# Deeper tile buffers and a new instruction order in a linear-attention and gated-MLP kernel on one core

## Chip, cores and metric

The kernel runs on one core of one Trainium2 chip. The metric is the device time of one execution in microseconds (us). Work on the core is spread over TensorE (PE), VectorE (DVE), ScalarE (ACT) and GpSimd (POOL); SyncE (SP) only issues transfers.

## What is computed

The input x has 2048 rows of 448 numbers in bfloat16. Two blocks follow each other, each with a layer norm in front and a residual addition behind:

```python
q, k, v = split(norm(x) @ wqkv)                 # 16 heads of 28
pq, pk = q @ w_phi, k @ w_phi                   # per head
phi_q = concat(softmax(pq), softmax(-pq))       # the same for phi_k
kv = phi_k^T v;  z = sum(phi_k over rows)       # per head
h = x + ((phi_q @ kv) / (phi_q @ z + 1e-6)) @ wo
h2 = h + (sigmoid(norm(h) @ w_gate) * (norm(h) @ w_up)) @ w_down   # 1792 hidden
```

## The kernel before, in words

The rows are cut into 16 tiles t of 128. Everything is one graph of tasks (class `_Graph`): a task has a name such as `("phi", 3)`, an engine or a choice of engines, one function that issues its instructions, and a list of tasks that it needs. `ORDER` (line 40) is a list of 902 numbers and fixes the order: number // 32 is the task by its place of creation, number % 4 says which of its allowed engines runs it, and number // 4 % 8 which PSUM banks it gets. `stored` (line 129) reads it, and `emit` (line 250) turns it into one in-order queue for each engine, with semaphore waits in front of an instruction where a task that it needs is on another engine or in a DMA. No engine skips a waiting instruction, SP's queue of transfers included. The bank gates are part of the waits: a product may write a bank pair only once the tasks that read its former content have ended (`until`).

The stages, with the names that the prediction uses:

- Opening. x, w_qkv's K, V and Q parts and w_phi are loaded (L461). PE runs `fill` products on zeros (L988, `NFILL` of them). `kT`/`WkT` (L540, L425) transpose the K weights, `Wp` on POOL or DVE (L524) spreads w_phi over the heads of a block, `wM`/`W2` (L555, L425) fold both into Wk and later Wq.
- Norm of x. Per tile `bst`, `agg` (bn_stats, bn_aggr, DVE, L583 and L585); per batch of tiles `ve` (L586), `rstd` (a power, POOL, L588), `mm`, `nm` (L591, L593); then `xn` (L602 or L603, ACT or DVE) writes the normalised tile into one of `NXP` slots of `xn_pad`. Tiles 0 to 3 are transposed by PE (`xP`, L613, with the copy `xT`, L425), the others two at a time by a DMA that SP issues (L621).
- K and V, and the key features. `pa`, `pb` (L637) are the first four and last three steps of a tile's K and V products, run as pairs on the two row halves of the array into a bank pair. `ekp`, `ekm` (ACT, L659 and L657) take exp of plus and minus K into one of `NEK` slots of `ek`; `v1` copies V into one of `NV` slots. `sa` (L667, POOL or DVE, written here as half_s) adds the two halves of each head, `ss` (L673) reduces, `rs` (L682) inverts, `phi` (L684) multiplies into one of `NPHI` slots, all but some `sa` on DVE. `kv` (PE, L696) accumulates phi and V over all tiles in bank 4, and `kvz` (L751) copies it out.
- Query features. `qa`, `q` (L736) for each of 4 chunks of 512 rows and 2 group pairs, `eqp`, `eqm` (ACT, L746).
- Read-out. `num` (PE, L772) per tile, `ocp` (L425, ACT or DVE, into opm), then on DVE per pair of tiles `rSm`, `rr`, `b`, `c`, `rd`, `o`, `od` (L788 to L819), a transpose `oT` (by PE for pair 0: `oP`, L808; by a DMA for the others, L821), `woa`, `wo_` (L833), and `h` (L863) or, for pair 0, `wr` and `hc` (L841, L856).
- Second norm. `bst2`, `agg2`, `ve2` (L871), `rstd2` (POOL, L873), `hn` (L877), `hT`.
- Gate/up and down. `ga`, `gu` (L934) into two banks, `sig` (ACT tanh, L943), `hh` (DVE, L951), `dn` (L968), `fin` (L975), store (L978). The gate and up weights (`wg`, `wu`, L461) come by eight SP loads, each behind a stage of the K products and behind the load two places before it in their list.

A slot of a buffer is written again only after its last reader: `xn` waits for the transpose `NXP` tiles back, `ekp` for the `phi` `NEK` back, `phi` for the `kv` `NPHI` back, `v1` for the `kv` `NV` back.

Of the kernel before, what the change touches and what calls it, by code (L numbers as in the profile page):

```python
# [5 lines left out]
dt = mybir.dt  # L6
ALU = mybir.AluOpType
# [3 lines left out]
P = 128  # L11
D = 448
H = 16
DH = 28
# [15 lines left out]
FIRST = [(0, 0), (0, 1), (0, 2), (0, 3), (1, 0), (1, 2), (1, 3)]  # L30
SECOND = [(1, 0), (1, 1), (1, 2), (1, 3), (0, 0), (0, 1), (0, 3)]
NWARM = 1
NFILL = 14

O_FIRST = [(0, 0), (0, 1), (0, 2), (0, 3), (1, 0), (1, 1), (1, 2)]
O_SECOND = [(1, 0), (1, 1), (1, 2), (1, 3), (0, 0), (0, 1), (0, 2)]
# [1 line left out]


ORDER = """  # L40
544 576 0 480 1152 609 224 737 128 28416 160 640 96 28448 352 801 192 28480 768 256 448 28512 384 896 28544
992 28576 1952 832 28608 28640 960 1984 2017 2112 28672 2048 673 28704 2144 705 2080 28736 2336 2176 928 28768
2208 2272 864 1184 1088 2368 2304 1316 2240 1216 2720 1120 1384 1344 1260 288 2656 1409 4144 2400 1588 512
1281 4160 2432 1440 1636 2592 1600 4072 9632 1472 2464 1520 28800 2496 1665 28832 4096 4204 1537 2528 4276
4225 1056 2624 4576 2688 2560 4289 2752 2785 3104 2848 2816 4608 3168 10272 3040 4516 5824 1024 2881 5536 2913
4712 2945 5568 3136 3200 3072 4320 2976 4544 3232 5632 4736 3264 5792 3008 5664 5888 4640 5696 6304 4352 5601
320 4672 6368 3297 5728 6336 5856 1760 5920 3328 1700 6080 1832 3616 5760 1793 3744 3360 4772 6048 3392 6112
3425 3680 6144 1888 3456 4800 5952 1856 3776 3648 4384 6400 3552 4832 1728 6176 6560 4904 5984 6592 10304 3488
4864 6208 6656 10176 6432 4928 6624 10208 3712 3584 6464 6848 4964 3809 6240 6816 6496 3520 6016 6272 3873
6881 6912 6528 7072 4416 4992 7136 6688 3840 7104 5024 6944 7392 10240 6720 5096 1921 6976 9664 3904 7360 6752  # L50
5056 9696 7328 7169 5120 3936 7008 10408 7616 3969 7584 7200 7424 4448 6784 7840 7040 7232 7648 10432 7680
7456 7904 5216 7488 7872 7264 10464 5160 7520 4032 7712 7936 5248 5184 7744 10496 9728 7776 7296 7552 4001
8096 7808 8161 4480 8128 5284 7968 8384 8352 5352 8193 10336 8416 8448 8224 5312 10144 8000 5376 8256 416 8608
8032 10532 8640 8672 8705 8864 8064 8480 10560 8896 8288 8928 5476 9792 10592 8736 8960 9760 5416 8512 8544
10624 5504 8768 5440 8992 9376 8800 10788 9408 9152 9024 9473 9120 8320 8576 9056 9184 8832 10816 9440 9504
9216 10656 9536 10848 9248 11048 9568 10880 9280 10688 9312 9088 10720 9344 9824 9600 9856 11072 11424 10752
10368 11524 12524 11104 11553 11456 11488 12545 12452 12480 13216 11584 13292 11616 11136 11648 10916 12576
13312 11680 11176 12608 12640 9888 13248 14060 10944 11712 12672 14080 11200 11744 10976 12704 11904 13344
11864 12736 11804 11232 13376 12768 11873 12800 11808 11008 13408 11936 13440 11264 13996 14756 13472 11968
13504 14016 11304 13536 12032 13568 12096 14112 14828 14784 12064 11328 12128 14144 12160 12000 14176 12836  # L60
12192 14848 12224 14208 15584 12864 12288 15616 12256 12408 12896 12348 13600 12353 14240 12416 12928 15524
13632 15552 14272 17836 13664 11360 17856 18084 14880 17888 17952 12992 11392 18112 17920 17984 13696 18476
9920 18144 18016 13024 18600 12960 14304 13728 13056 14336 18048 18496 13088 18176 18624 13760 18528 18208
18656 18560 18340 18688 18240 13792 13152 16364 9952 18272 18728 13825 13120 16384 18368 18304 13856 13184
18752 14912 18400 18976 13920 18784 16300 18432 19008 13888 14372 18816 19040 13952 14944 16320 17064 14400
19072 14976 9984 19232 14432 18860 17088 19264 18880 16416 19492 18912 19368 18944 19520 15008 16448 19392
19552 20076 19424 19584 15648 20196 15040 15072 19456 15104 20096 14464 19944 15680 20128 10016 19296 20224
19328 10048 20160 19968 20256 20448 20000 20032 20588 20288 15144 16480 17124 15712 15168 10080 17152 20608
15200 10112 20480 20640 20708 20672 20512 15744 19112 19820 15232 16512 20736 20544 19136 15776 20768 19840
16544 19168 21344 19200 15808 20328 19872 20800 19904 21220 14528 20352 15296 20844 15264 16576 20384 14496  # L70
15328 20416 21248 15360 15392 14560 20864 21280 15840 15456 21480 15872 20896 21312 20928 21376 14593 20964
14624 21408 21100 14656 21440 20992 16608 15424 16640 17184 21120 21024 17216 14688 15904 17248 21152 15488
21056 21504 15936 14720 21536 19620 19712 19648 21184 21568 15968 21996 19744 22248 22496 22016 22528 22048
22272 22080 22116 17280 22304 22560 17312 16684 22336 22592 22144 22632 22176 22208 16704 23136 16736 22756
17344 22656 16768 16832 22784 22688 23168 22720 22816 23660 23200 22376 23232 23680 16800 22848 22880 16000
16032 16864 22400 16064 22912 22432 21796 22464 16096 17376 16128 22944 16160 23712 16192 23744 21608 22976
16897 16224 16928 16256 16960 21696 17408 21632 16992 21664 17024 21888 23020 21920 21728 23264 21824 23040
23400 23296 17444 23328 23072 23424 23360 17472 32 23104 23456 24544 23488 17504 24300 25320 24320 24804 24352
24384 24576 25344 24608 24832 24640 25068 17600 24864 24896 24160 25088 25376 25828 25408 25120 25152 24680
25856 23532 25888 25920 24192 17536 23552 24224 17632 24704 24256 23584 25188 24736 25568 24768 25216 17568  # L80
23616 17664 24936 17696 25248 25280 25600 24428 25632 25664 25700 17728 24448 17760 24960 24480 25728 24512
23776 25760 24992 23980 23808 23840 21760 17792 23872 24064 23904 25792 25024 24000 26464 24096 26596 26496
26984 26528 26624 26560 27116 26656 27008 26688 26720 27040 25444 27072 27496 27136 26752 27168 27520 26784
27200 25472 27552 26816 27584 28012 25504 26336 25536 27240 28032 26368 28064 27748 26400 27264 26432 27776
28096 27296 26848 27328 27372 26880 27808 27880 26912 27840 27392 26944 27620 27904 27424 27648 64 27456 26144
27680 27936 25964 26240 25984 26016 26048 26272 27968 26304 27712 26176 28136 26080 26112 19680 21952 23936
28224 24032 28160 21856 26208 28320 19776 28256 24128 28288 28192 28352 28384
"""


# [5 lines left out]
class _Graph:  # L96
# [29 lines left out]
    def opt(self, name):  # L126
        return name if name in self.tasks else None
# [186 lines left out]
def dve(cycles):  # L314
    return 0.07 + cycles / 960.0
# [6 lines left out]
def build(nc, A_x, A_wqkv, A_w_phi, A_wo, B_w_gate, B_w_up, B_w_down, out):  # L322
# [13 lines left out]
    out_t = out[0].rearrange("(n p) d -> p n d", p=P)  # L336
    wd_v = B_w_down.rearrange("(ft p) n -> p ft n", p=P)

    NXP, NEK, NPHI, NV, NOP, NO, NHP, NSG, NSA = 8, 4, 3, 4, 3, 2, 2, 4, 2
    SPLIT = range(NT)  # L340

    with ExitStack() as es:
        es.enter_context(nc.allow_low_precision("bf16 factors of bf16 products"))

        def sb(name, shape, d=dt.bfloat16):
            return es.enter_context(nc.sbuf_tensor(name, shape, d))
# [39 lines left out]
        wd_sb = sb("wd_sb", [P, FT, D])  # L386
        ssum = sb("ssum", [P, NEK, 2 * H], dt.float32)
        rsum = sb("rsum", [P, NEK, 2 * H])
        half_s = sb("half_s", [P, NSA, D], dt.float32)
        v1 = sb("v1", [P, NV, H, EV])  # L390
        eq = [sb("eq%d" % c, [P, 2, G, 512]) for c in range(NCH)]
        kvz = sb("kvz", [P, 2, G, E, 2])
# [4 lines left out]
        rden = sb("rden", [P, 2, 2, G, HL])  # L397
        o_pad = sb("o_pad", [P, NO, 2, 512])
        oT = sb("oT", [P, NO, 2, G, P])
# [11 lines left out]
        K = _Graph(nc)  # L411
        task, opt = K.task, K.opt
# [165 lines left out]
        PE_X = (0, 1, 2, 3)  # L578
        VV = (0,)
        batches = [(0, 1), (1, 2), (2, 4), (4, 8), (8, 12), (12, 16)]  # L580
        for (a, z) in batches:
# [12 lines left out]
                    nm1[:, a:z], nm1[:, a:z], rs1[:, a:z], ALU.mult), [("rstd", a), ("mm", a)], engs=("pool", "dve"))  # L594
            for t in range(a, z):
                s = t % NXP
                free = opt(("xT", (t - NXP) // 2 * 2)) or opt(("xT", t - NXP))

                def f(e, t=t, s=s):
                    dst, src = xn_pad[:, s, :].rearrange("p (a n) -> p a n", a=2), lap(X(t))  # L600
                    if hasattr(e, "activation"):
                        return e.activation(dst, src, ACT.Identity, bias=nm1[:, t:t + 1], scale=rs1[:, t:t + 1])  # L602
                    return e.tensor_scalar(dst, src, mv1[:, t, 0:1], rs1[:, t:t + 1], op0=ALU.subtract, op1=ALU.mult)  # L603
                task(("xn", t), None, dve(160), f, [("rstd", a), opt(("nm", a)), free],
                     engs=("dve",) if a < 4 else ("act", "dve"))
# [155 lines left out]
        for pr in range(NPR):  # L761
            t0 = 2 * pr
            c = t0 // 4
            sp_, s2 = pr % NOP, pr % 2
# [21 lines left out]
            def fac(a, n):  # L786
                return a[:, :, :, None, :].to_broadcast([P, 2, G, n, HL])
# [11 lines left out]
                rden[:, s2], b_sb[:, s2, :, :, EV - 1, :]), [("c", pr), opt(("o", pr - 2))])  # L799
            task(("o", pr), "dve", dve(448), lambda e, pr=pr, s2=s2, fac=fac: e.tensor_tensor(  # L800
                o_pad[:, pr % NO, :, 0:D].rearrange("p t (g d j) -> p t g d j", g=G, j=HL), b_sb[:, s2, :, :, 0:DH, :],
                fac(rden[:, s2], DH), ALU.mult), [("rd", pr), opt(("oT", pr - NO))])
            if pr in PE_O:
                for j in range(2):
                    def f(e, pr=pr, j=j):
# [115 lines left out]
        for c, (t0, n) in enumerate(CH):  # L921
# [33 lines left out]
            for t in range(t0, t0 + n, 2):  # L955
                pr = t // 2
# [29 lines left out]

        for i in range(NFILL):
            task(("fill", i), "pe", 0.22, lambda e: e.matmul(  # L988
# [40 lines left out]
```

## Time and profile before

| | us |
|---|---|
| median of 3 runs (lowest, highest) | 208.22 (207.96, 210.22) |
| the profiled execution | 207.67 |
| span of its instructions | 205.9 |
| PE, DVE, ACT, POOL busy | 197.2, 135.6, 96.5, 30.6 |
| granted TensorE clock, mean | 1.000 |

The span runs from the first to the last instruction. A line of an engine's instructions in order of time has the start, the duration, the engine, the line of the code, the operation, the tile written and those read, sizes, and the count of merged instructions; in brackets stands the idle time before it and what ended it. Instructions of one engine overlap a little at their ends, so the step from one start to the next is shorter than the duration. For a DMA the issue is shown, and its landing is told apart.

### The profile page before, as it was taken

How to read it: one execution, taken by the hardware profiler on the slowest of the kernel's cores; microseconds unless marked ns; L12 is line 12 of the kernel's file. 1: busy time of each engine (PE TensorE's matmuls, PEld its weight loads, DVE VectorE, ACT ScalarE, POOL GpSimd, SP SyncE). 2: the span in 40 equal slices, each digit the busy share in tenths (PEclk: the TensorE clock that was granted, in tenths of full speed). 3: DMA queues.
4: the chain of work that ended last, by engine and by line, in shares of the span. 5: the costliest groups of instructions: out<-in, count | busy, mean ns of one | idle time of the engine just before them, and what ended most of it. 6: DMA issues, size and time to landing. Idle time of an engine off the chain costs nothing.

```text
span 205.9 us, 5431 instructions
## 1 busy us (share of the span) xinstructions
PE 197.2 (96%) x2278; PEld 107.1 (52%) x2278; DVE 135.6 (66%) x312; ACT 96.5 (47%) x172; POOL 30.6 (15%) x56
## 2 busy tenths in 40 slices
PE   7899998998988999999999999999999999999993
PEld 2544555455445876554444444544444455796553
DVE  2999999997998996789823875435446415351241
ACT  2579999799998773443311333003334400442000
POOL 3738653420003110001100001100001000000000
PEclk9999999999999999999999999999999999999999
DMA  5996477764022493700450000620000031000034
GB/s 167 279 277 128 76 188 200 181 223 142 3 57 48 73 173 81 197 3 3 94 111 3 0 0 3 124 51 0 3 0 5 2 79 20 0 3 0 25 111 156
DMA packets 35109, 16.94 MB, mean 82 GB/s; under 512 B 26828, under 2 KB 34060, under 8 KB 35084
## 3 DMA queue, kind: packets, MB, share of 16 engines
q1 hardware_dynamic: 34140, 15.78, 33.1%
q10 hardware_dynamic: 944, 0.80, 1.4%
q8 instruction: 18, 0.29, 0.6%
q14 instruction: 7, 0.06, 0.1%
HBM read 8.98 MB, written 1.84 MB: 53 GB/s over the span
## 4 chain that ended last, share of the span: by engine, by line
PE 78%; DVE 12%; ACT 4%; DMA 2%; issue 1%; POOL 1%
PE bank L934 42%; PE bank L968 21%; PE bank L637 5%; PE bank L833 4%; PE bank L736 3%; DMA x_sb<-in_A_x_dram 2%; DVE phi L684 2%; PE bank L696 1%; DVE ssum L673 1%; DVE xn_pad L603 1%; DVE st L583 1%; ACT xn_pad L602 1%; ACT ek L659 1%; DVE b_sb L792 1%; DVE b_sb L795 1%
## 5 line engine op out<-in xcount | busy, mean ns | idle before, releaser
L934 PE MATMUL bank<-xnT,wg_sb 64*128 64x512 bf16 (+1 forms) x490 | 87.4, 333 | 0.1
L934 PE MATMUL bank<-xnT,wu_sb 64*128 64x512 bf16 (+1 forms) x490 | 87.4, 333 | 0.0
L943 ACT ACTIVATE sg_sb<-bank 128x512 f32<-128x512 f32 (+1 forms) x70 | 34.6, 513 | 77.9 <-PE bank L934 74.0
L951 DVE SCALAR_TENSOR_TENSOR hh<-sg_sb,bank 128x512 bf16<-128x512 f32 (+1 forms) x70 | 39.1, 576 | 28.4 <-ACT sg_sb L943 28.1
L934 PEld LDWEIGHTS bank<-xnT,wg_sb 64*128 64x128 bf16 x490 | 45.3, 94 | 21.9 <-issue 1.9
L934 PEld LDWEIGHTS bank<-xnT,wu_sb 64*128 64x128 bf16 x490 | 45.1, 94 | 15.5
L968 PE MATMUL bank<-wd_sb,hh 128*128 128x448 bf16 (+1 forms) x238 | 43.1, 342 | 0.0
L968 PEld LDWEIGHTS bank<-wd_sb,hh 128*128 128x128 bf16 x238 | 22.9, 98 | 20.1 <-issue 1.4
L975 DVE SCALAR_TENSOR_TENSOR x_sb<-bank,x_sb 128x448 bf16<-128x448 f32 (+1 forms) x17 | 9.9, 594 | 28.3 <-PE bank L968 28.3
L637 PE MATMUL bank<-Wk,xnT 64*128 64x448 bf16 x112 | 22.1, 350 | 0.4 <-ACT Wq L425 0.3
L637 PE MATMUL bank<-Wv,xnT 64*128 64x448 bf16 x112 | 21.6, 350 | 0.0
L746 ACT ACTIVATE eq<-bank 128x1024 bf16<-128x1024 f32 x16 | 16.3, 1067 | 0.7 <-PE bank L736 0.6
L871 POOL TENSOR_SCALAR rs<-mv 128x2 f32<-128x2 f32 x5 | 1.3, 256 | 99.6 <-DVE mv L869 50.3
L667 POOL TENSOR_TENSOR half_s<-ek 128x448 f32<-128x448 bf16 x12 | 12.9, 1078 | 15.3 <-ACT ek L657 7.0
L425 ACT CAST opm<-bank 128x960 bf16<-128x960 f32 x14 | 13.7, 1014 | 2.8 <-PE bank L772 2.1
L833 PE MATMUL bank<-wo_sb,oT 64*128 64x448 bf16 x112 | 13.3, 350 | 0.9 <-DVE oT L425 0.6
L736 PE MATMUL bank<-xnT,Wq 64*128 64x512 bf16 x112 | 14.0, 377 | 0.1
L637 PEld LDWEIGHTS bank<-Wk,xnT 64*128 64x128 bf16 x112 | 9.1, 94 | 6.9 <-PE bank L637 1.0
L637 PEld LDWEIGHTS bank<-Wv,xnT 64*128 64x128 bf16 x112 | 9.2, 94 | 4.3
L684 DVE TENSOR_TENSOR phi<-ek,rsum 128x896 bf16<-128x896 bf16 x16 | 10.3, 655 | 0.3 <-PE bank L696 0.2
L583 DVE BATCH_NORM_STATS2 st<-x_sb 128x6 f32<-128x448 bf16 x16 | 9.4, 612 | 1.7 <-DMA x_sb<-in_A_x_dram 1.7
L657 ACT ACTIVATE ek<-bank 128x448 bf16<-128x448 f32 x16 | 9.7, 630 | 1.3 <-PE bank L637 1.3
(91 smaller groups left out, 185.4 us busy)
## 6 DMA issues: line engine op xcount, KB each, us to landing
wg_sb<-in_B_w_gate_dram SPq DMA_DIRECT2D x4, 448.0 KB, 3.8
wu_sb<-in_B_w_up_dram SPq DMA_DIRECT2D x4, 448.0 KB, 3.7
out_dram<-x_sb SPq DMA_DIRECT2D x15, 112.0 KB, 1.8
wd_sb<-in_B_w_down_dram SPq DMA_DIRECT2D x7, 224.0 KB, 2.7
x_sb<-in_A_x_dram SPq DMA_DIRECT2D x2, 448.0 KB, 5.8
wq_raw<-in_A_wqkv_dram SPq DMA_DIRECT2D x4, 128.0 KB, 5.3
x_sb<-in_A_x_dram SPq DMA_DIRECT2D x2, 224.0 KB, 4.5
x_sb<-in_A_x_dram ACTq DMA_DIRECT2D x2, 224.0 KB, 4.9
```

The costliest lines, as they stand in the source:

```text
L425: return e.copy(dst, src) if hasattr(e, "activation") else e.tensor_copy(dst, src)
L583: task(("bst", t), "dve", dve(D), lambda e, t=t: e.bn_stats(st1[:, t % 4, :], X(t)), [x_ld[t], opt(("agg", t - 4))])
L637: r = e.matmul(bank[bk][:, 0:D], lhsT=half(xnT, hi)[:, t, k, :], rhs=half(w, hi)[:, k, :], start=(i == 0), stop=(i == 6), tile_position=(6 ...
L667: task(("sa", t), None, 0.88, lambda e, t=t, s=s: e.tensor_tensor(half_s[:, t % NSA].rearrange("p (a n) -> p a n", a=4 * G), ek[:, s].rear ...
L684: task(("phi", t), None, 1.68, lambda e, t=t, s=s: e.tensor_tensor(phi[:, t % NPHI, :, :, 0:DH, :].rearrange("p a g d h -> p (a g) d h"), ...
L736: r = e.matmul(bank[bb[j]], lhsT=half(Wq2, hi)[:, k, 2 * g:2 * g + 2].rearrange("p c d h -> p (c d h)"), rhs=half(xnT, hi)[:, 4 * c:4 * c ...
L746: task((key, gp, c), "act", act_p(1024), lambda e, gp=gp, c=c, sg=sg, nm=nm: e.activation(eq[c][:, sg, 2 * gp:2 * gp + 2, :], wide[got(nm) ...
L833: r = e.matmul(bank[bb[j]][:, 0:D], lhsT=half(oT, hi)[:, pr % NO, j, k, :], rhs=half(wo_sb, hi)[:, k, :], start=(i == 0 and not res), stop ...
L934: r = e.matmul(bank[b][:, 0:N], lhsT=half(w, hi)[:, k, fs], rhs=half(hnT, hi)[:, t0:t0 + n, k, :], start=(i == 0), stop=(i == 6), tile_pos ...
L943: task(("sig", f_, c), "act", act_p(N), lambda e, j=j, N=N, nm=nm: e.activation(sg_sb[:, j % NSG, 0:N], bank[got(nm)[0]][:, 0:N], ACT.Tanh ...
L951: task(("hh", f_, c), "dve", dve(N), lambda e, j=j, N=N, nm=nm, f_=f_, c=c: e.scalar_tensor_tensor(hhT[c % 2][:, f_, 0:N], sg_sb[:, j % NS ...
L968: r = e.matmul(bank[b][:, c0:c1], lhsT=hhT[c % 2][:, f_, o:o + P], rhs=wd_sb[:, f_, c0:c1], start=(f_ == 0), stop=(f_ == FT - 1))
```

## The change

Four buffer depths grow: normalised tiles, exps, key features, values. Three fills are added. A slot's release in `xn` is named more exactly, the form of `xn` is chosen by the task's engine, and `o` gets the waits on the PE transposes of pair 0. The table `ORDER` is another one, of 905 numbers.

```diff
-NFILL = 14
+NFILL = 17
...
 ORDER = """
-544 576 0 480 1152 609 224 737 128 28416 160 640 96 28448 352 801 192 28480 768 256 448 28512 384 896 28544
...
+544 576 0 224 352 1152 609 480 28416 768 288 28448 256 640 28480 512 384 128 96 448 28512 736 320 160 28544
...
-    NXP, NEK, NPHI, NV, NOP, NO, NHP, NSG, NSA = 8, 4, 3, 4, 3, 2, 2, 4, 2
+    NXP, NEK, NPHI, NV, NOP, NO, NHP, NSG, NSA = 10, 6, 6, 6, 3, 2, 2, 4, 2
...
-        half_s = sb("half_s", [P, NSA, D], dt.float32)
+        half_s = sb("half_s", [P, NSA, D], dt.float32) if len(SPLIT) else None
...
-                free = opt(("xT", (t - NXP) // 2 * 2)) or opt(("xT", t - NXP))
+                free = opt(("xT", t - NXP if t - NXP in PE_X else (t - NXP) // 2 * 2))
...
-                    if hasattr(e, "activation"):
+                    if K.tasks[("xn", t)].eng == "act":
...
-                fac(rden[:, s2], DH), ALU.mult), [("rd", pr), opt(("oT", pr - NO))])
+                fac(rden[:, s2], DH), ALU.mult), [("rd", pr), opt(("oT", pr - NO)), opt(("oT", pr - NO, 0)), opt(("oT", pr - NO, 1))])
```

What the new table does to the engines, counted from its numbers:

| task | before | after |
|---|---|---|
| `xn` | 9 DVE, 7 ACT | 12 DVE, 4 ACT |
| `v1` | 3 DVE, 13 ACT | 4 DVE, 12 ACT |
| `W2` | 8 ACT | 7 ACT, 1 DVE |
| `xT` of tiles 0 to 3 | 2 DVE, 2 ACT | 1 DVE, 3 ACT |
| `sa` | 12 POOL, 4 DVE | 14 POOL, 2 DVE |
| `phi` | 16 DVE | 15 DVE, 1 POOL (tile 12) |
| `oT` of pair 0 | 2 DVE | 1 DVE, 1 ACT |
| `hc` | 2 ACT | 1 ACT, 1 DVE |
| `ve`, `nm` | 4 + 1 DVE, 2 + 2 POOL | 3 + 0 DVE, 3 + 3 POOL |
| `ve2` | 3 DVE, 5 POOL | 7 DVE, 1 POOL |
| x loads | 4 SP, 2 ACT | 6 SP |

And to the order, in the parts that the prediction speaks of:

- PE: 12 fills stood before the first `kT` and 2 before `xP 2`; now 10 stand before it, 2 among the folds, 4 before `xP 2` and 1 behind `xP 3`. `kv 6` to `9` and `kv 10` to `15` are run in one go each. The first three products of the gate/up stage are of other hidden tiles, and one `num` stands behind the first `ga`.
- DVE: `bst` of tiles 0, 1, 3, 2, 7, 6, 5 stood before `xn 2`; now those of all tiles 0 to 7 do. The last steps before `kvz` are now `v1 15`, `v1 14`, `ss 12`, `rs 12`, `sa 14`, `ss 14`, `ss 15`, `rs 14`, `rs 15`, `phi 14`, `phi 15`. In the read-out `b 3` and `c 3` now stand behind the first `hn`.
- POOL: tile 1's `rstd`, then both `Wp`, then tile 0's `ve` and `rstd`. The last work of the stage is `sa 13`, `sa 12`, `sa 15`, `phi 12`.
- ACT: `eqp`, `eqm`, `ocp` and the pair 0 copies are interleaved in another way.
- SP: the load `wg 3` stands behind the transpose `oT 1`, where it stood ahead of it. Of Wv's two loads, the second stands behind all of Wq's.

## The prediction

> **What bounds the kernel now.** I read the busy shares and the 40 slices first, then the busy time by stage, then the instructions in order of time on VectorE (DVE), ScalarE (ACT), GpSimd (POOL) and TensorE (PE) for the stages that are not full.
>
> ```profile
> PE 197.2 (96%) x2278; PEld 107.1 (52%) x2278; DVE 135.6 (66%) x312; ACT 96.5 (47%) x172; POOL 30.6 (15%) x56
> ...
> DVE  2999999997998996789823875435446415351241
> ACT  2579999799998773443311333003334400442000
> ```
>
> DVE and ACT are full for the first third of the span and loose afterwards. The stages have their ends where PE's work changes: first K/V product at 11.76, last at 42.73, first read-out product (L772) at 49.38, first gate/up product (L934) at 66.45.
>
> ```profile
> 0.00:11.76 11.76, 9.74 (x66) 4.99 (x66) 7.58 (x21) 5.29 (x10) 5.76 (x22) 1.00 0.92 236
> 11.76:42.73 30.97, 29.99 (x430) 15.35 (x430) 30.10 (x77) 28.67 (x57) 15.97 (x20) 1.00 0.75 173
> 42.73:49.38 6.65, 6.65 (x140) 3.46 (x137) 5.41 (x11) 6.00 (x10) 1.39 (x1) 1.00 0.67 218
> 49.38:66.45 17.07, 14.65 (x300) 7.92 (x299) 15.75 (x38) 16.18 (x21) 1.62 (x2) 1.00 0.17 33
> 66.45:205.95 139.50, 136.19 (x1354) 75.32 (x1350) 76.73 (x168) 40.38 (x78) 5.82 (x11) 1.00 0.22 49
> ```
>
> Columns: stretch and length, then busy PE, PEld, DVE, ACT, POOL. From 66.45 PE runs dense to its last product (136.19 of 139.50; about 3.2 is the closing addition and store), with DVE at 55% and ACT at 29%. So the time is what comes before 66.45 plus a fixed 139.5, and only PE's idle time before it can be won.
>
> PE's overlapping records overstate how full it is, so I take steps from start to start. A tile's K and V products take 0.76 + 0.57 = 1.33 us, a q product 0.86 + 0.65 = 1.51, a kv step 0.27 (0.1 more where the array changes its row split), a read-out 0.23. From 11.76 to 42.73 that is 16 x 1.33 + 2 x 1.51 + 10 x 0.27 + four folds at 0.2 + some 12 changes at 0.1 = 29.0 of 30.97: 2.0 idle. From 42.73 to 49.38 PE is dense. From 49.38 to 66.45 the same count gives 12.8 of 17.07: 4.3 idle. The most that can be won is about 6, besides the opening.
>
> VectorE ends the middle: its last phi ends at 47.80, kv follows, and the first read-out starts 1.58 later. Some of its time is lost to POOL:
>
> ```profile
> 27.75 0.61 DVE L667 TENSOR_TENSOR half_s<-ek 128x448 f32<-128x448 bf16 x1
> ...
> 28.81 1.06 DVE L603 TENSOR_SCALAR xn_pad<-x_sb,mv,rs 128x512 bf16<-128x512 bf16 x1
> ...
> 31.57 1.87 DVE L684 TENSOR_TENSOR phi<-ek,rsum 128x896 bf16<-128x896 bf16 x2
> ```
> ```profile
> 28.49 1.23 POOL L667 TENSOR_TENSOR half_s<-ek 128x448 f32<-128x448 bf16 x1 [1.52 <-ACT ek L657]
> 30.54 0.97 POOL L667 TENSOR_TENSOR half_s<-ek 128x448 f32<-128x448 bf16 x1 [0.82 <-ACT ek L657]
> 31.79 1.16 POOL L667 TENSOR_TENSOR half_s<-ek 128x448 f32<-128x448 bf16 x1 [0.28 <-ACT ek L659]
> ```
>
> An xn takes 0.41 elsewhere and 1.06 here, a phi 0.62 elsewhere and 1.39 as the second of the pair at 31.57, and both end where POOL's half_s ends. POOL's own 0.97 becomes 1.23 and 1.16 behind a phi. With the xn at 7.79 (1.03, beside Wp on POOL) DVE loses 0.62 + 0.65 + 0.78 = 2.05.
>
> **The change part by part.**
>
> Opening. The two x loads on ACT's queue go to SP's. The loads that land up to 12.73 in the trace are the same set in another order, and they land as their bytes go through, so Wv (last but for x 12-15 now) comes at about 12.7 and the first V product needs it at 13.3: nothing, but with only 0.6 of cover. Ten fills instead of twelve stand before the kT transposes, so these may start near 5.5 instead of 6.35; that chain ends in Wk, which no longer decides. DVE decides: eight bn_stats (step 0.53) instead of seven now stand before xn 2 and 3, but one xnT copy (0.33) goes to ACT and xn 1 no longer meets Wp (0.62). My count has xn 2 at 10.65 and xn 3 at 10.97, as in the trace. Four fills (0.22 each) now stand between the last fold (about 10.3) and xP 2, and one behind xP 3: first K product at 12.07, +0.3. Ends: -0.3 (the fills hidden and DVE ahead) and +1.0 (both Wp, 1.08 together, and their wait for w_phi now stand before tile 0's rstd on POOL).
>
> The larger buffers. Their memsets on POOL are larger (phi's 0.42 doubles, v's 0.37 grows by half: +0.6), hidden in POOL's idle 2.9 before rstd. A phi no longer waits for the kv three tiles back (0.2 in the trace), an exp for the phi four back. The bank gates stay.
>
> ScalarE, exps from 13.54 until the evacuation of tile 11 ends, 22.6 solid. It issues xn at step 0.71 and exps, v copies and folds at 0.42. Of seven xn there three stay (one goes ahead of the first exp): -2.84; one v copy more, one fold copy fewer. 22.6 becomes 19.8. PE needs 12 x 1.33 + 6 x 0.27 + 1.51 + 1.2 of folds and changes = 20.6 there, so PE becomes its own limit and the 2.0 idle may go: last K/V product at 12.07 + 29.0 = 41.1 instead of 42.73. By the bank gates pa 4 waits some 0.4 for DVE's fold copy; the other banks come free 0.2 or more ahead of need.
>
> VectorE until the last phi, in steps: three xn more (+1.0), one v copy (+0.55), one fold copy (+0.53), one xnT copy less (-0.33), one phi (-0.53), two half_s (-1.06), one ve and one nm (-0.3): -0.1. So its own work, 43.34 - 2.05 - 0.8 idle = 40.5, stays, and could end at 44.9. But the last two v copies wait for PE at 41.1; behind the second stand ss, rs 12, half_s 14, ss 14 and 15, two rs, two phi: 4.8 in steps from 41.3, so 46.1. That leaves about 0.8 of slack for meetings with POOL earlier.
>
> POOL gets fourteen half_s instead of twelve and phi 12. Before shows no phi on POOL. Lower end 0.97 (the half_s row: the same operands read), upper end 1.94 (that row by outputs, 896 to 448). I take 1.9, since a POOL Wp (224 outputs, 0.54) follows outputs too. It becomes ready at 42.8, after rs 12, when half_s 14 becomes ready on DVE. If DVE is first, POOL runs from 43.2 to 45.1 and phi 14 on DVE, due at 44.9, hardly waits. If POOL is first, DVE's last phi ends at 48.0. Meetings elsewhere cost 1.4 in this stretch before; the same 1.4 less the slack is 0.6. I take last phi 46.9 (46.1, 0.6 and a little), kept ends 46.1 and 48.6. With the 1.58 behind it, first read-out at 48.5: -0.9.
>
> The Trainium skill ("SBUF — State Buffer", section "SBUF: two separate sides") says that the port pair which VectorE shares with GpSimd is an exclusive lock: whichever starts first holds it for its whole instruction, a VectorE operation with two SBUF inputs included. By that rule, the trace agrees (1.06 for 0.41, 1.39 for 0.62), and it speaks against more POOL work with SBUF operands; free sharing would put the last phi at 46.1, the lock with POOL first at 48.0.
>
> From the first read-out to the first gate/up product DVE chains rSm, rr, b, c, rd, o for pairs 0 to 2 and the first norm. From rSm 0 (51.96) the first hn started 11.79 later, the second 0.33 after. Now one oT copy (0.33) goes to ACT, b 3 and c 3 (0.67 each) stand behind the first hn, ve2 goes from POOL (0.51, with hops) to DVE (0.15); one hc copy (0.53) comes onto DVE, under POOL's rstd2 (1.10). First hn after 10.5, second after 11.5: 0.6 earlier. ACT then carries both hT behind two exps and an opm copy, and the first ga waits for h 1 on DVE, so I keep 0.45, less 0.25 where the third ga waits for h 2: -0.2. Ends -0.6 and +0.4.
>
> SP issues wg 3 behind the transpose oT 1, which waits for od 1 on DVE: on my count issued at 57.9, landed by 62 (3.8 in the trace), needed at about 65.1. Nothing, cover 3.
>
> Gate/up stage: the same products, one read-out more inside than ahead (counted), four more ve2 of 0.1 on a DVE with 45% free: 0, within 0.3 each way.
>
> Sum: -0.9 - 0.2 = -1.1. The profiled execution took 207.67 around a span of 205.9, so 206.6 in its terms; the median shown is 208.22, 0.55 above, so 207.1.
>
> **The rivals.**
>
> PE's whole idle goes. Last phi at 46.1, less the opening's 0.3, is 45.8; with 1.58 behind it the first read-out comes at 47.4, so -2.0, and the later part at its end of -0.6 makes -2.6: 205.6. For it: ACT's 2.8. Against it: PE, ACT and DVE would all have to run with no slack.
>
> VectorE keeps its end. Its work is unchanged by 0.1, and meetings as costly as before hold the last phi at 47.8: 208.0.
>
> The port decides against the change. POOL's phi gets in before half_s 14, and fourteen half_s cost DVE as much as twelve: 48.6, first read-out 50.2, +0.8 with nothing won behind it: 209.0; with a second such meeting of 1.9, 210.9. It decides from a last phi later than 47.9. For it: the two become ready within 0.1 of each other. Against it: half_s 14 stands right behind rs 12 on DVE, while POOL hears of rs 12 through a semaphore.
>
> Gate/up waits for wg 3. If od 1 slips by more than 3, or a load as long as xT's longest (5.2) meets it, the stage starts late by the excess: 208 to 211.
>
> **How the numbers follow.** Forecast 0.42, whole idle 0.25, VectorE's end 0.10, port 0.17, wg 3 0.06. Under 1% (2.1 us) a measurement hardly tells from no change. Faster by more takes the whole-idle case and the forecast's edge: 0.27. Slower by more takes half of the port case and most of wg 3: 0.12. The rest, 0.61, is within. The likeliest case alone spans 206.2 to 208.0; the range of 8 in 10 is 205.2 (the whole idle, with 0.3 and a little from the gate/up stage) to 209.8 (the port case with part of a second meeting).
>
> **What would show it.** First K product near 12.1; last K/V product near 41.1; fewer and shorter ACT gaps; POOL's phi of 1.9 after 43; last DVE phi near 46.9; first read-out 48.5; first ga 65.1. Wrong would be: a first K product past 12.8, a phi or xn on DVE over 1 us more than three times, a half_s on DVE of over 2 us at 43, or PE idle at L934 with SP as releaser.

## The result and the profile after

The changed kernel takes 209.52 us (median of 20 runs, lowest 207.88; one at 712.83 stands far outside all the others), the kernel before 207.68 in 20 runs (207.17 to 210.22). The ratio, taken from the fast runs alone (all but the outlier) and not from the two medians, is 1.0079, 95% interval 1.0063 to 1.0096: slower by 0.8%, or 1.6 us. The time lies inside the range given and the change within 1%, but on the other side of zero from the forecast of 1.1 us less. The forecast of 207.1 and its range stood on the 208.22 that three runs of the kernel before gave; with the 207.68 of twenty they would lie 0.5 lower, at 206.6 and up to 209.3, so that the time falls inside the range is luck.

The profiled execution took 210.0 around a span of 208.3. Its busy times and slices:

```profile
PE 197.2 (95%) x2281; PEld 109.1 (52%) x2281; DVE 137.0 (66%) x315; ACT 95.3 (46%) x168; POOL 33.2 (16%) x57
...
DVE  2898899997999796678877467622575162442132
ACT  2688997778999566334303323300244210342000
```

PE's work is the same 197.2, so the 2.4 that the span grew by is idle time of PE. ACT has become looser, as intended: in the stretch of the K and V products below it is idle for 4.6, where it was for 2.3. DVE's slices there are still full. By stage, with the same ends as in the prediction (first and last K/V product, first read-out, first gate/up product; columns as there):

```profile
0.00:12.45 12.45, 10.57 (x67) 5.46 (x68) 7.83 (x26) 6.08 (x11) 7.05 (x26) 1.00 0.85 234
12.45:44.81 32.36, 29.39 (x429) 15.55 (x430) 30.79 (x70) 27.75 (x54) 17.52 (x21) 1.00 0.77 183
44.81:51.24 6.43, 6.43 (x141) 3.47 (x138) 5.45 (x12) 5.26 (x8) 2.90 (x2) 1.00 0.13 45
51.24:69.17 17.93, 14.57 (x284) 7.74 (x283) 16.17 (x39) 16.73 (x21) 0.70 (x1) 1.00 0.37 57
69.17:208.30 139.13, 136.19 (x1370) 76.86 (x1368) 76.77 (x170) 39.49 (x77) 5.03 (x8) 1.00 0.20 49
```

The K/V stretch is 32.36 instead of 30.97 and the read-out 17.93 instead of 17.07; the other two are a little shorter (6.43 for 6.65, 139.13 for 139.50). The opening's 12.45 is this execution's own: VectorE idles 0.86 for an x load, and in the eight executions of this order and its variants that the experiments add, the first K product comes at 11.45 to 11.73. What PE waits for, summed over the span (us in total, times, longest):

```profile
PE bank L696 <- DVE phi L684: 1.9, 2, 1.4
PE bank L833 <- DMA oT<-o_pad: 1.5, 1, 1.5
...
PE bank L555 <- DMA WqT<-wq_raw: 1.0, 1, 1.0
```

In the view of before the two DMA waits do not stand, and the one for phi is smaller:

```profile
PE bank L696 <- DVE phi L684: 0.6, 1, 0.6
```

The two DMA waits are for transposes, and each transpose has something new ahead of it in SP's queue. SP's own instructions at both places (start, duration), first in the opening, then in the read-out, and behind them the same places before:

```profile
8.61 1.01 SPq L461 DMA_DIRECT2D Wv<-in_A_wqkv_dram  x1
9.66 1.57 SPq L461 DMA_DIRECT2D wo_sb<-in_A_wo_dram  x2
11.29 0.43 SPq L461 DMA_DIRECT2D x_sb<-in_A_x_dram  x1
11.84 3.37 SPq L501 DMA_TRANSPOSE WqT<-wq_raw  x2
```
```profile
59.52 1.29 SPq L821 DMA_TRANSPOSE oT<-o_pad  x1
60.91 0.51 SPq L461 DMA_DIRECT2D wg_sb<-in_B_w_gate_dram  x1
62.02 1.24 SPq L821 DMA_TRANSPOSE oT<-o_pad  x1
```
```profile
10.92 1.33 SPq L501 DMA_TRANSPOSE WqT<-wq_raw  x1
12.30 0.94 SPq L461 DMA_DIRECT2D wo_sb<-in_A_wo_dram  x1
13.36 1.25 SPq L501 DMA_TRANSPOSE WqT<-wq_raw  x1
...
57.23 4.41 SPq L821 DMA_TRANSPOSE oT<-o_pad  x2
```

In the opening, two loads of W_o (`wom 6` and `wom 4`, the tile wo_sb) hold SP for 1.57 ahead of the load of x 12 and the transposes of Wq, which are issued at 11.84 and 13.29 (10.92 and 13.36 before) and land at 17.83 and 18.57 (14.98 and 17.13 before). In the read-out, `oT 2` is issued 1.1 behind the load `wg 3` and takes 5.5 to land, at 67.54; the tile's view gives its seven transposes 2.7 at the least, 2.8 in the middle, 5.5 at the most, and before 3.0, 3.1, 3.9. PE's two waits end there:

```profile
18.61 0.76 PE L555 MATMUL bank<-Wp,WqT 112*128 112x112 bf16 x12 [1.02 <-DMA WqT<-wq_raw]
...
67.59 0.93 PE L833 MATMUL bank<-wo_sb,oT 64*128 64x448 bf16 x8 [1.52 <-DMA oT<-o_pad]
```

The third wait, for phi, comes from VectorE's meetings with POOL: moments at which both work and one holds the other up. Both engines in order of time (start, duration):

```profile
23.84 0.94 DVE L586 TENSOR_SCALAR rs<-mv 128x4 f32<-128x4 f32 x1
...
29.19 1.38 DVE L603 TENSOR_SCALAR xn_pad<-x_sb,mv,rs 128x512 bf16<-128x512 bf16 x2
...
31.98 1.98 DVE L684 TENSOR_TENSOR phi<-ek,rsum 128x896 bf16<-128x896 bf16 x2
...
36.79 1.91 DVE L684 TENSOR_TENSOR phi<-ek,rsum 128x896 bf16<-128x896 bf16 x2
...
39.53 1.30 DVE L684 TENSOR_TENSOR phi<-ek,rsum 128x896 bf16<-128x896 bf16 x1
```
```profile
23.54 1.22 POOL L667 TENSOR_TENSOR half_s<-ek 128x448 f32<-128x448 bf16 x1 [0.28 <-DVE ssum L673]
...
28.91 1.19 POOL L667 TENSOR_TENSOR half_s<-ek 128x448 f32<-128x448 bf16 x1 [2.69 <-ACT ek L659]
31.18 2.28 POOL L667 TENSOR_TENSOR half_s<-ek 128x448 f32<-128x448 bf16 x2 [1.09 <-DVE ssum L673]
...
37.23 0.98 POOL L667 TENSOR_TENSOR half_s<-ek 128x448 f32<-128x448 bf16 x1 [0.33 <-ACT ek L657]
39.38 0.97 POOL L667 TENSOR_TENSOR half_s<-ek 128x448 f32<-128x448 bf16 x1 [1.16 <-DVE ssum L673]
```

Each of the five DVE rows holds one instruction that starts beside a `half_s` of POOL and ends shortly behind its end (0.03 for `ve`, 0.16 for xn, 0.48 for phi): `ve` 12 takes 0.94 (0.16 for the same line and form at 11.76), the xn of tile 15 1.06 (0.41), three phi about 1.3 to 1.4 (0.62). In the two pairs of phi the first runs free and the second is held. That is 0.78 + 0.65 + 0.77 + 0.77 + 0.68 = 3.65 of VectorE's time in the middle, where before lost 0.65 + 0.77 = 1.42. The last phi starts at 49.08.

PE meets the late phi long before the last one. In its queue `kv 4` and `kv 5` stand behind phi 4, which ends at 33.95, and `kv 8` and `kv 9` behind phi 8, which ends at 40.83; PE's rows there, and the only such row of before:

```profile
34.01 0.69 PE L696 MATMUL bank<-v,phi 128*64 128x58 bf16 x32 [0.51 <-DVE phi L684]
...
40.88 0.69 PE L696 MATMUL bank<-v,phi 128*64 128x58 bf16 x32 [1.37 <-DVE phi L684]
```
```profile
35.07 0.44 PE L696 MATMUL bank<-v,phi 128*64 128x58 bf16 x16 [0.57 <-DVE phi L684]
```

From there on PE is late by itself: `kv 10` to `kv 15` follow a q product without a gap, and `kv 15` starts at 50.08, 0.39 behind the end of the last phi.

### The profile page after: what moved, and what is told of

Its sections match the earlier page's. It is cut to its first block, busy times and chain, and to the rows that moved or that the text cites. A ratio compares the mean times of both kernels' runs of the same rounds, so it can differ in the third digit from the quotient of the medians.

```text
span 208.3 us, 5442 instructions
## 1 busy us (share of the span) xinstructions
PE 197.2 (95%) x2281; PEld 109.1 (52%) x2281; DVE 137.0 (66%) x315; ACT 95.3 (46%) x168; POOL 33.2 (16%) x57
## 4 chain that ended last, share of the span: by engine, by line
PE 74%; DVE 12%; SPq 6%; DMA 5%; issue 2%
PE bank L934 41%; PE bank L968 21%; SPq L461 5%; PE bank L833 4%; DVE phi L684 3%; DMA oT<-o_pad 3%; PE bank L637 3%; PE bank L736 3%; DMA WqT<-wq_raw 3%; DVE ssum L673 2%; PE bank L696 1%; DVE xn_pad L603 1%; DVE rsum L682 1%; PE bank L772 1%; DVE o_pad L800 1%
## 5 line engine op out<-in xcount | busy, mean ns | idle before, releaser
L873 POOL TENSOR_TENSOR rs<-rs,neghalf 128x2 f32<-128x2 f32 x8 | 5.5, 697 | 103.5 <-DVE rs L871 103.5
L637 PE MATMUL bank<-Wk,xnT 64*128 64x448 bf16 x112 | 21.5, 350 | 0.1
L637 PE MATMUL bank<-Wv,xnT 64*128 64x448 bf16 x112 | 21.0, 349 | 0.0
L667 POOL TENSOR_TENSOR half_s<-ek 128x448 f32<-128x448 bf16 x14 | 14.9, 1067 | 15.0 <-ACT ek L657 7.1
L833 PE MATMUL bank<-wo_sb,oT 64*128 64x448 bf16 x112 | 13.3, 350 | 1.7 <-DMA oT<-o_pad 1.5
L425 ACT CAST opm<-bank 128x960 bf16<-128x960 f32 x14 | 13.2, 996 | 2.0 <-PE bank L772 2.0
L637 PEld LDWEIGHTS bank<-Wv,xnT 64*128 64x128 bf16 x112 | 9.7, 94 | 6.1
L684 DVE TENSOR_TENSOR phi<-ek,rsum 128x896 bf16<-128x896 bf16 x15 | 11.2, 770 | 0.1
L673 DVE TENSOR_REDUCE ssum<-half_s 128x32 f32<-128x448 f32 x16 | 9.4, 593 | 0.0
```

Source lines behind the costliest of these rows:

```text
L425: return e.copy(dst, src) if hasattr(e, "activation") else e.tensor_copy(dst, src)
L637: r = e.matmul(bank[bk][:, 0:D], lhsT=half(xnT, hi)[:, t, k, :], rhs=half(w, hi)[:, k, :], start=(i == 0), stop=(i == 6), tile_position=(6 ...
L667: task(("sa", t), None, 0.88, lambda e, t=t, s=s: e.tensor_tensor(half_s[:, t % NSA].rearrange("p (a n) -> p a n", a=4 * G), ek[:, s].rear ...
L673: task(("ss", t), "dve", dve(448), lambda e, t=t, s=s: e.tensor_reduce(ssum[:, s, :].rearrange("p (a h) -> p a h", h=2), half_s[:, t % NSA ...
L684: task(("phi", t), None, 1.68, lambda e, t=t, s=s: e.tensor_tensor(phi[:, t % NPHI, :, :, 0:DH, :].rearrange("p a g d h -> p (a g) d h"), ...
L833: r = e.matmul(bank[bb[j]][:, 0:D], lhsT=half(oT, hi)[:, pr % NO, j, k, :], rhs=half(wo_sb, hi)[:, k, :], start=(i == 0 and not res), stop ...
```

## The experiments

Theory: three prices add up. SP's queue delays the transposes of Wq (about 1) and `oT 2` (about 1), and VectorE loses about 2 more to POOL than before. Rivals: the two waits are only where a general lateness shows, so that mending them brings another wait; the larger buffers or the additional phi on POOL cost the time. Where nothing else is said, the compared kernel before ran on the same chip beside it.

### wg 3 ahead of the transpose (e1_wg3_ahead)

```diff
 SP's queue, read-out
+wg 3
 oT 1
-wg 3
 oT 2
```

> The changed kernel with one transfer moved: the load wg 3 is issued ahead of the transpose oT 1 on SP, as it stood before the change, and nothing else. Theory A (the transpose oT 2 lands 5.5 us after its issue, at 67.54, because the 448 KB of wg 3 go through ahead of it, and PE waits 1.5 for it at woa 2): oT 2 lands near 65.1, the wait is gone, the first gate/up product comes 1.3 to 1.5 earlier (near 67.8), time near 208.0 to 208.2. Rival (oT 2 is late because DVE ends o 2 late, and the first gate/up product is held by h 1 on DVE, which ends at 67.17, or by hT): less than 0.5 is won.

Measured: 208.05 against 207.38, ratio 1.0032 (1.002 to 1.0044), where the unchanged kernel had 1.0079. `oT 2` is issued at 61.24 and lands at 63.95; the slowest of the seven takes 3.6. The transposes stand in one row, with nothing between, and the read-out stage is 16.69 (17.93 unmended):

```profile
58.74 3.73 SPq L821 DMA_TRANSPOSE oT<-o_pad  x2
```
```profile
50.46:67.15 16.69, 14.67 (x283) 7.64 (x282) 15.95 (x39) 16.60 (x21) 0.70 (x1) 1.00 0.15 33
```

About 1.0 of the 1.6 us lies here (0.75 if the 1.0068 of e9 is taken for the changed kernel). The wait is not replaced: no DMA holds L833 in this execution.

### The transposes of Wq ahead of W_o (e2_wqt_early)

```diff
 SP's queue, opening
-wom 6, wom 4
 x 12
 wqT 1, wqT 0
 ...
 xT 8
+wom 6, wom 4
```

> The changed kernel with the two loads wom 6 and wom 4 moved on SP from ahead of x 12 to behind the transpose xT 8; nothing else. Theory A (the transposes of Wq land 6.0 and 5.3 after their issue, the second at 18.57, because they stand behind wom and x 12 in the queue; PE waits 1.0 for it, and DVE waits 0.53 and 0.77 for PE's products behind that): the second lands near 17, PE's wait is gone, the two DVE waits shrink by most of 1.3, and the last phi, the first read-out and the end come about 1.0 earlier: 208.5. Rival (the middle is set by DVE's meetings with POOL, and what is won at 18 is given back to them): the wait at 18 goes, but the first read-out moves by less than 0.4.

Measured: 207.91 against 207.38, ratio 1.0031 (1.0019 to 1.0043): another 1.0 (0.8 against 1.0068). Both transposes go out earlier:

```profile
9.07 0.47 SPq L461 DMA_DIRECT2D x_sb<-in_A_x_dram  x1
9.87 3.34 SPq L501 DMA_TRANSPOSE WqT<-wq_raw  x2
```
```profile
PE bank L833 <- DMA oT<-o_pad: 1.7, 1, 1.7
...
PE bank L555 <- DMA WqT<-wq_raw: 0.2, 1, 0.2
```

They land at 14.43 and 16.83, and PE's wait for them falls to 0.2, while the wait for `oT 2`, which this kernel keeps, stands. That the W_o loads lengthen the transposes themselves is only partly so: they still need 4.6 to 5.4 to land (5.3 to 6.0 unmended). The gain comes from issuing them earlier: beside e1 and e9, whose openings are like this one, the second is issued 1.2 earlier and lands 1.0 earlier. In this execution the meetings of phi 9 and phi 8 did not happen either (phi 11 lost 0.32 instead), and PE has no wait for phi but a new one of 0.8 for `xT 10`, which takes 5.6 to land. So its first read-out, at 48.32, is no measure of the edit; its time, 207.32, is the lowest of its six runs.

### Both (e3_both_sp)

The two edits together.

> Both moves on SP together. If the two waits are separate in time they add up: 1.4 and 1.0 off the changed kernel's time, near 207.1, about the kernel before. If the second theory of either holds, 0.5 less or more.

Measured: 207.0 against 207.38, ratio 0.9988 (0.998 to 0.9997). The two savings add up (0.47% and 0.48%, together 0.91%), and neither is given back. The rest of the distance to the forecast is in the K/V stretch:

```profile
11.71:43.12 31.41, 29.48 (x430) 15.49 (x431) 30.78 (x70) 27.53 (x54) 17.58 (x21) 1.00 0.79 185
...
49.54:66.22 16.68, 14.67 (x282) 7.63 (x281) 15.94 (x39) 16.59 (x21) 0.70 (x1) 1.00 0.15 33
```

It is 31.41 long, longer than before's 30.97, with all five meetings in it and the same two waits of PE for phi (0.50 and 1.37).

### The larger buffers with the old order (e4_deep_old_order)

```diff
 changed kernel
-NFILL = 17
+NFILL = 14
 ORDER: the table of the kernel before
```

> The deeper buffers alone: the changed kernel's code with the order and the fills of the kernel before. Theory (the depths are not what binds in the order before, 0.2 of waits in all): within 0.3 of the kernel before, 207.4 to 208.0. Rival (POOL's larger memsets or the places of the buffers in memory cost): slower by 0.5 or more. Other rival (the depth was what bound): faster by 0.5 or more.

Measured: 207.13 against 207.38, ratio 0.9989 (0.998 to 0.9997). The buffers cost nothing and by themselves are worth about 0.1%; the loss is the order's (the three fills went back with it).

### POOL's additions replaced by writes (e5_half_memset)

On top of both SP edits. The halves' sums that POOL would form are left out of the computation; POOL writes a constant into `half_s` instead, so it reads no SBUF there.

```diff
-task(("sa", t), None, 0.88, lambda e, t=t, s=s: e.tensor_tensor(
+task(("sa", t), None, 0.88, lambda e, t=t, s=s: e.memset(half_s[:, t % NSA].bitcast(dt.bfloat16), 1.0) if K.tasks[("sa", t)].eng == "pool" else e.tensor_tensor(
```

> Base: both SP moves (207.0). POOL's fourteen half_s additions are replaced by a memset of the same tile, 896 elements of 16 bits, about 0.87 us each: POOL is about as long on the same tile at the same places, but reads no SBUF. This leaves the sums out of the computation. Theory A (DVE's stretched operations are held by POOL's hold on the port that both share, and for an operation with two SBUF inputs only against a POOL operation that reads SBUF): the phi of 1.3 to 1.4 go back to 0.62, the xn at 27.5 may stay long; 2.2 to 3.2 of stretch go, the last phi ends 1.5 to 2.5 earlier than 48.0, limited by PE's last V product, and the time falls to about 205.0 to 205.8. Rival 1 (any POOL operation, by its write, holds DVE): stretches stay near 0.5 each. Rival 2 (DVE's stretch is a wait for data or the end is set by ACT or PE): the time moves by less than 0.4.

Measured: 205.21 (204.69 to 205.74). On this chip the kernel before ran from 207.73 to 210.1, so the ratio (0.983, 0.9776 to 0.9883) says less than the comparison with the next kernel, which ran on the same chip and is as fast as the two SP edits alone: 206.96, so 1.75 less. The four runs lie at 204.7 and 205.7, two each, and the profiled one is the fastest; its span is 2.3 less, all of it before the first read-out:

```profile
11.62:40.79 29.17, 29.06 (x429) 15.39 (x430) 27.58 (x70) 27.29 (x54) 14.62 (x21) 1.00 0.78 183
...
47.22:63.90 16.68, 14.66 (x282) 7.63 (x281) 15.94 (x39) 16.59 (x21) 0.70 (x1) 1.00 0.18 44
```

The K/V stretch is now 29.17, by the prediction's count PE's own limit (29.0), and PE waits for no phi. VectorE's and POOL's instructions at the places of three of the meetings, and the tile phi (minimum, median, maximum in ns):

```profile
26.98 1.33 DVE L603 TENSOR_SCALAR xn_pad<-x_sb,mv,rs 128x512 bf16<-128x512 bf16 x2
...
29.70 1.14 DVE L684 TENSOR_TENSOR phi<-ek,rsum 128x896 bf16<-128x896 bf16 x2
...
33.56 1.08 DVE L684 TENSOR_TENSOR phi<-ek,rsum 128x896 bf16<-128x896 bf16 x2
```
```profile
27.16 1.01 POOL L667 MEMSET half_s<- 128x896 bf16 x1 [3.21 <-ACT ek L659]
...
29.90 0.84 POOL L667 MEMSET half_s<- 128x896 bf16 x1 [0.17 <-DVE ssum L673]
```
```profile
L684 DVE TENSOR_TENSOR phi<-ek,rsum x15: 556/614/626, 19.3 to 45.1; 128x896 bf16<-128x896 bf16 x15
```

POOL still works beside the pair of phi at 29.70, and yet no phi of this execution takes more than 0.626. The xn beside the write at 27.16 is still held (1.01 for 0.41). What holds a phi is thus something that the addition does and the write does not: the addition reads SBUF, and it also computes, which this run does not tell apart. The Trainium skill ("SBUF — State Buffer", section "Who interferes with whom") draws the same line: a VectorE instruction with two SBUF inputs is held up by a GpSimd instruction that reads SBUF and not by one that only writes it, and `tensor_scalar`, xn's form, can be in a mode that any GpSimd instruction excludes; the trace agrees on both, with 0.626 and 1.01. The writes are also shorter than the additions (0.84 for 0.97), so how much of the 1.75 is due to that is open.

### Phi 12 back on VectorE (e6_phi12_dve)

```diff
 on top of both SP edits
-POOL: sa 15, phi 12
+POOL: sa 15
+DVE: phi 12, behind sa 14
```

> Base: both SP moves (207.0). Phi 12 is given back to DVE, at its place. The prediction's port rival put up to 1.9 on POOL's phi 12; the traces show it 1.94 long, with half_s 14 ahead of it. Theory A (POOL's phi costs nothing where it stands): DVE gets 0.53 more in front of the last phi, time +0.2 to +0.6, about 207.4. Rival (POOL's phi holds DVE's last two phi): time falls by 0.3 or more.

Measured: 206.96, span 205.3, first read-out at 49.46; with phi 12 on POOL 207.0 (on another chip), 205.3 and 49.54. Neither the loss nor the gain came: the move of phi to POOL cost nothing and won nothing. VectorE's last phi does end 0.4 later behind the first K product (36.68 for 36.30), but with phi 12 on POOL `kv 15` started only 0.38 behind the last phi, because PE had its other kv products to do; now it starts 0.06 behind it. In the changed kernel `half_s` 14 came first on VectorE, as the prediction took it (46.47, ahead of POOL's phi 12 at 46.63, which took 1.94).

### Two xn to ScalarE (e7_xn_on_act)

```diff
 on top of both SP edits
-DVE: xn 15, xn 14
+ACT: xn 15 (behind v1 8), xn 14 (behind v1 11)
 SP's queue
-xT 14
 wg 0, wu 1
+xT 14
```

> Base: both SP moves (207.0). xn 15 and xn 14 go from DVE to ACT, behind v1 8 and v1 11 where ACT has gaps of 0.2 to 1.7, and the transpose xT 14 behind wu 1. Theory A (DVE's queue sets the end of the middle): DVE loses 0.33 twice and the 0.65 of the xn beside POOL's half_s, so its last phi comes about 1.0 to 1.3 earlier, if another meeting does not take its place: 205.8 to 206.2. Rival (PE or ACT set it): no gain, or a loss from the later evacuations of tiles 11 and 10, 207.0 to 207.6.

Measured: 205.46 (205.04 to 205.91) beside the 206.96 of the kernel above: 1.5 less, more than expected, with the computation whole. The K/V stretch falls to 29.95 and the rest stays:

```profile
11.45:41.40 29.95, 29.43 (x431) 15.35 (x432) 29.04 (x68) 28.75 (x56) 17.07 (x21) 1.00 0.77 173
41.40:47.80 6.40, 6.40 (x140) 3.44 (x137) 5.43 (x12) 5.24 (x8) 2.91 (x2) 1.00 0.54 166
47.80:64.48 16.68, 14.66 (x282) 7.62 (x281) 15.94 (x39) 16.59 (x21) 0.70 (x1) 1.00 0.22 59
```

ScalarE's six xn take 0.81 to 0.86, the two beside POOL's additions included. ScalarE had the time: with the two SP edits alone it is idle for 3.9 in that stretch. The meeting of the xn is gone, and the phi meet POOL at other moments: phi 4, 7 and 11 are held by 0.77, 0.44 and 0.45, with `ve` 12 2.4 together instead of 3.65, and PE waits for none of them.

### Before with wg 3 late (e8_before_wg3_late)

```diff
 the kernel before, SP's queue
-wg 3
 wom 7, wu 3
 oT 1
+wg 3
 oT 2
```

> The kernel before with one transfer moved the other way: wg 3 is issued behind the transpose oT 1. Theory A (a transpose waits for the bytes of the load issued ahead of it): oT 2, issued at 60.40 and landed at 63.43 before, lands up to 2.4 later, at 65 to 66; woa 2, due at 64.87, waits up to 0.9: 208.0 to 208.4, from 207.4. Rival (the load itself is what would be late): wg 3 lands at 62, ahead of its need at 66.4, so no change.

Measured: 209.52 against 208.68, ratio 1.0013 (0.9954 to 1.0071), with before's wide spread on this chip: inconclusive as a time. The trace shows the mechanism without the price: `oT 2` takes 4.7 to land (3.1 is the least of its seven), but PE waits for it only 0.2, since before's order uses it later. In this execution the first K product came at 13.94, behind late loads.

### The changed kernel again (e9_after_again)

No edit.

> The changed kernel as it is, once more, beside the kernel before on the same chip. The profiled execution of the change had its first K product at 12.45, and the runs with only SP moves had it at 11.5 to 11.7, with x 4 landed at 6.1 instead of 7.0. If that is a chance of the opening and not of the change: here it is near 11.6, the span is 0.8 under 208.3, and the ratio to before stays at 1.005 to 1.009 by the three losses alone (the transposes of Wq, the transpose oT 2, the meetings on the shared port). If the opening is what the change costs: 12.4 again.

Measured: 209.06 against 207.39, ratio 1.0068 (1.0044 to 1.0092). By this ratio the change costs 1.4, and each of the two SP edits saves about 0.75 and not 1.0. The same waits are there: the transposes of Wq 1.3, `oT 2` landing in 5.3 with 1.3, 3.6 of meetings. One is new: `oT 3`, issued at 72.2, needs 5.6 and holds PE for 0.7 more behind L833, so that the last stage is 140.2 long. The first K product is at 11.57.

### Ve 12 to POOL (e10_ve_on_pool)

```diff
 on top of the two xn on ScalarE
-DVE: ve 12, mm 12
+POOL: ve 12, mm 12
```

> Base: both SP moves and xn 15 and 14 on ACT (ratio 0.984). ve 12 and mm 12 go from DVE to POOL, ahead of half_s 5, so that ve 12, 0.16 long alone and 0.94 beside half_s 5, no longer stands on DVE. Theory A (DVE sets the end of the middle, and a tiny DVE operation is held by POOL's as long as a large one): DVE is rid of 0.9 of steps, the last phi comes up to 0.9 earlier, limited by PE's last V product near 40.8 with 4.8 behind it, so 0.1 to 0.6 off the time: ratio 0.981 to 0.984. Rival (the meeting only moves to the next phi): no change within 0.2.

Measured: 205.22 against 207.39, ratio 0.9902 (0.988 to 0.9923); span 203.6, first read-out at 47.83 (47.80 without the edit). `ve` is no longer held, but the work that follows comes at other moments and meets POOL elsewhere, so that the loss is 2.4 as without the edit:

```profile
28.82 2.15 DVE L684 TENSOR_TENSOR phi<-ek,rsum 128x896 bf16<-128x896 bf16 x2
```
```profile
27.28 3.20 POOL L667 TENSOR_TENSOR half_s<-ek 128x448 f32<-128x448 bf16 x3 [2.48 <-ACT ek L659]
```

Here both phi of a pair are held, 2.15 for 1.16 together. The meeting moved, and nothing is won over the kernel with two xn on ScalarE. In both PE waits for no phi, `kv 10` to `kv 15` follow a q product, and `kv 15` starts 0.38 behind the last phi, so an earlier last phi had nothing to bring forward. These two kernels are faster than both given ones.

## Why the prediction was wrong

The sum, taken apart in the spans (forecast 204.85, that is 205.95 less 1.1; profiled 208.3), with the execution of both SP edits (205.3) between them:

| step | forecast | both SP edits | unmended |
|---|---|---|---|
| first K product | 12.07 | 11.71 | 12.45 |
| from there to the last phi's end | 34.83 | 36.30 | 37.24 |
| from there to the first read-out | 1.6 | 1.53 | 1.55 |
| read-out stage | 16.87 | 16.68 | 17.93 |
| gate/up stage | 139.5 | 139.08 | 139.13 |

- **Opening.** "+0.3" for the fills was too dear: 11.45 to 11.73 in eight executions. The fills are hidden. But the part of this step that was called "nothing" failed: it looked at when Wv lands and left out what else had been moved on SP's queue. The two W_o loads, 1.57 of SP, stand ahead of x 12 and the transposes of Wq. PE waits 1.0 to 1.3 behind them, and e2 gives 1.0 of the time back. The instruction order of SP was there to be read; the landing of `WqT` against its use (17.13 against 17.8 before, so 0.7 of cover) was left out.
- **ScalarE** did become loose, and PE's idle time could go, as said: where VectorE is not held the stretch is 29.17 (e5), against 29.0 forecast. In the kernel as changed it is 32.36: about 1.0 more for the transposes of Wq (31.41 in e3) and 2.2 more because VectorE holds PE up.
- **VectorE and the port.** The work and the free end were right: from the first K product to the last phi's end the forecast had 34.0 without meetings (46.1 less 12.07), and e5 has 34.05. The term "the same 1.4 less the slack is 0.6" was mis-sized: 3.65 instead of 1.42, and the last phi ends 2.3 later than without (36.30 less 34.05). The path was not the one of the sum either. It let the meetings eat the slack in front of the last phi; but PE pays for them at `kv 4` and `kv 8`, which wait 1.9 for held phi (0.57 before), then everything behind is late, the last V product and with it the last phi, and `kv 15` starts 0.38 to 0.39 behind that phi. Costs of meetings were carried over from the order before, though which instructions meet is a matter of moments: in the new order three phi, an xn and even a 4-element `ve` do.
- **POOL's phi** took 1.94 for the estimated 1.9, half_s 14 came first as taken, and it cost nothing (e6).
- **Read-out.** "-0.2" was -0.39 once `oT 2` lands in time (e3).
- **wg 3.** "Nothing, cover 3" is the step that failed outright. The cover was that of the load's own landing, and that held: it landed at 64.60. Not counted was what stands behind it on its queue: `oT 2` is issued 1.1 later, takes 2.5 more to land than it took before (5.5 for 3.0), and is used at once. e1 gives 1.0 back (0.75 by e9's ratio).
- **Gate/up** stayed fixed, 139.13 for 139.5, as said.

In time: -1.1 forecast, +1.0 for the transposes of Wq, +1.0 for `oT 2`, and 0.85 by which e3 falls short of the forecast by its ratio (-0.25 instead of -1.1), together +1.75; measured is +1.6, and +1.4 in e9. Of the rivals, "the port decides" had the right resource and the wrong place (phi 12 against half_s 14, where nothing was lost), and "gate/up waits for wg 3" the right move and the wrong victim.

Two workings of the prediction are off without bearing on this: 12 x 1.33 + 6 x 0.27 + 1.51 + 1.2 is 20.3 and not 20.6, and before's held xn and phi end 0.15 and 0.48 behind POOL's `half_s` and not with it.

Open: how the changed kernel's spread (207.88 to 210.37 without the outlier) divides into meetings that happen or not (e2), transposes that land late (`oT 3` in e9, `xT 10` in e2) and late loads in the opening; and whether the two best kernels (e7, e10) differ at all, which ran on different chips.

## What to carry to other kernels

When a load is moved on a queue, price it by what stands behind it there, above all by transposes whose result is used at once, and not only by its own landing. Two engines that hold each other up, as VectorE and POOL do here, lose time by the moment at which their instructions meet, so a new order needs a new count of meetings and not the old one's, and it matters who waits for each held instruction: here products in the middle of PE's queue did, and not the last one. In pairs of phi back to back POOL's addition came in between and held the second. The surer cure was to move some of the work to an engine that had time and was not held: ScalarE's two xn took 0.83 and 0.86 beside POOL's additions, its others 0.81 to 0.84.

## What the runs showed of the hardware

- `oT 2` lands in 4.7 to 5.7 in the four executions in which a 448 KB load was issued ahead of it on the same queue (e8, e9, the changed kernel, e2), 2.8 to 3.2 behind the landing of that load, and in 2.7 to 3.0 in the eight others. It is not a fixed price: `xT 10`, issued 0.6 to 2.5 behind a load of the same size in the new order, took 3.1 to 5.6. `oT 3` took 5.6 once (e9) with nothing but a load issued 1.3 behind it, which the other executions have too; why, is open. In the opening, with other loads still landing, the transposes of Wq need 3.3 to 6.0.
- An instruction of 4 elements per partition (`ve`, 0.16 alone) took 0.94 beside one POOL addition: it ends 0.03 behind the addition, so its loss was what was left of the addition.
- A POOL write of `half_s` took 0.84 alone and held an xn (1.01 for 0.41) and `ve` 12 (0.54 for 0.16) but none of fifteen phi.
